# A third output buffer and two moved groups of row sums in a fused attention and mixture-of-experts kernel

## The chip, the cores and the metric

The kernel runs on one core of one Trainium2 chip. The metric is the device time of one execution in microseconds (us); less is better.

## The reference, cut to what matters

```python
# q, k, v: 8 batches, 8 heads, 576 tokens, 64 wide; s: one number per token and head
scores = (q @ k.T) / sqrt(64)                       # causal
scores += minimum(-(cum_i - cum_j), 0)              # cum = cumsum(max(s, 0))
x = softmax(scores) @ v                             # all heads side by side: (4608, 512)
logits = x @ w_gate                                 # 8 experts
# a token keeps the expert of the token before it unless its local gate says "fresh"
e = argmax(logits[t]) if first or sigmoid(x @ w_local) < 0.5 else e_of_the_token_before
out[t] = softmax(logits)[e] * (maximum(x[t] @ w1[e], 0) @ w2[e])   # w1: 512x1024, w2: 1024x512
```

All numbers are 32-bit floats.

## The kernel before, in words

The kernel has two stages. The first, attention with the routing of tokens to experts, takes about the first 205 us. It writes each token's row of x into a table in DRAM that is sorted by expert, with indirect DMAs from GpSimd's queue (`put`, L371). The change doesn't touch it.

The second stage (`Experts`) works through 17 **units**, numbered 0 to 16, in the order `PPDDDDDDDDXTXDMXD`. A unit is a block of rows that belong to one expert: P and D have 256 rows, X is a wide unit of 464 rows, T and M are made of smaller pieces with weights of their own. Each unit has two **phases**: layer 1 (h = relu(x w1)) and layer 2 (y = h w2, times the gate). The phases are interleaved, so that layer 1 of unit u+1 stands between layer 1 and layer 2 of unit u: 1(0), 1(1), 2(0), 1(2), 2(1), and so on, to 1(16), 2(15), 2(16). This document writes 1(13) for layer 1 of unit 13.

Most phases are computed as a 2x2 block product with seven block products instead of eight (`layer_split`, L738 on): all phases of D and X units, and layer 2 of P units. TensorE makes the products in the order p1, p2, p6, p7, p5, p4, p3 (each in a PSUM bank, X units in layer 1 in two). Around them stand these helper operations:

- **Row sums** (`row_sums`, L691): three additions over blocks of the left operand. For x (layer 1) they write the tile xSs and the block a21 of xTs, for h (layer 2) the tile hSs and the block a21 of hT. On GpSimd (POOL) for all but the first units: lines 700, 701, 702. p6 and p5 read the sums, p7 reads the new a21. The tiles hSs and xSs have two halves, used by units of even and odd number in turn; a wide unit takes both halves (`half_of`).
- **The fourth sum** (`row_fourth`, L704, L706): subtracts a sum from the block a12, also on POOL. It can run only when p2 has read the old a12, and p3 needs the new one.
- **Weight sums** (`weight_first` to `weight_fourth`, L655): four subtractions on VectorE (DVE) over blocks of the weights. p5 needs the first, p6 the second, p7 the third, p4 the fourth.
- **The combination** (`add`, L759): DVE adds products from PSUM to running sums. p1 is copied to the tile sa by ScalarE (ACT, L776); p6 gives sb, p7 gives sc; the four results c11, c22, c21, c12 go to hT (layer 1) or to an output tile y (layer 2). ACT then applies relu (L767) or the gate (L763).
- **The stores**: in layer 2 each finished row block of y goes to DRAM by an indirect DMA from POOL's queue (`store`, L818 to L825), which waits for ACT. Row block 1 (c21, c22) is stored after p4, row block 0 after p3. A unit takes one y tile, a wide unit two; the pool yp has two buffers, and a buffer is free again when its store has landed.

T and M units are not split in this way: layer 1 is L837, layer 2 L869 with its own product, and the output's scaling by the gate is L871.

The engines run freely and wait for each other by semaphores; each executes its own instructions in the order in which the program issues them. So an instruction that waits on POOL holds up all that stands behind it in POOL's queue. `run` writes this order out by hand: `job(phase, unit, i, f)` puts the helper f of some unit at place i of a phase; place i of a split phase comes after p1 (0), p2 (1), p6 (2), p7 (3), p5 (4), p4 (5) or p3 (6), and "pre" ahead of all. The helper `at(1)` is called right after `row_fourth` has been issued.

In this order the sums of h of unit u stood at place 0 of 1(u+1), and for the last unit, 16, at place 5 of 2(15).

Of the kernel before, what the change touches and what calls it, by code (L numbers as in the profile page):

```python
# [9 lines left out]
F32 = mybir.dt.float32  # L10
# [7 lines left out]
P = 128  # L18
B, H, S, DH = 8, 8, 576, 64
D = H * DH  # L20
E, F = 8, 1024
# [496 lines left out]
class Experts:  # L518
# [172 lines left out]
    def row_sums(self, u, layer):  # L691

        t, s, of = ((self.xT, self.xss, self.xS), (self.hT, self.hss, self.hS))[layer]
        t = t[u]
        n, h = t.shape[1] // 2, self.width(u) // 2
        s = self.half_of(s, u)[:, : 2 * n * h].rearrange("p (i c t) -> p i c t", i=2, c=n)
        s1, s2 = of[u] = [s[:, i] for i in range(2)]
        (a11, _), (a21, a22) = self.rows_of(t, u)
        on = self.adder(u, layer)
        on.tensor_tensor(s1, a21, a22, op=Alu.add)  # L700
        on.tensor_tensor(s2, s1, a11, op=Alu.subtract)  # L701
        on.tensor_tensor(a21, a11, a21, op=Alu.subtract)  # L702
# [35 lines left out]
    def layer_split(self, u, layer, at):  # L738

        nc = self.nc  # L740
        h, w, parts = self.width(u) // 2, D // 2, self.deep(u)
        p = h // parts
        if layer == 0:
            pool = self.hx if self.kind(u) == "X" else self.fp
            self.hT[u] = pool.tile([P, FK, 2 * h], F32, name="hT")
            (c11, c12), (c21, c22) = self.rows_of(self.hT[u], u)
        else:
            gi = self.gi.pop(u)
            ys = [self.yp.tile([P, 2, D], F32, name="y") for _ in range(parts)]
            y = [ys[r] if parts == 2 else ys[0][:, r : r + 1] for r in range(2)]  # L750
            (c11, c12), (c21, c22) = [[y[r][:p, :, i * w : i * w + w] for i in range(2)] for r in range(2)]

        def sums(name):
            s = self.sp.tile([P, FK // 2 * WIDE // 2], F32, name=name)
            return s[:p, : parts * w].rearrange("p (c w) -> p c w", c=parts) if layer else s[:, : 4 * h].rearrange("p (m t) -> p m t", t=h)

        def add(to, ps, s):
            for c, part in ps:
                nc.vector.tensor_tensor(to[:, c], part, s[:, c], op=Alu.add)  # L759

        def gated(to, r):
            for c in range(parts):
                ins = nc.scalar.mul(to[:, c], to[:, c], gi[:p, parts * r + c, 1:2]).ins  # L763
            return ins

        def last(to, r):
            return gated(to, r) if layer else nc.scalar.activation(to, to, Act.Relu).ins  # L767

        def store(r):
            for c in range(parts):  # L770
                self.store(y[r][:, c], gi, parts * r + c, p)

        p1 = self.product(u, layer, 1)
        s1 = sums("sa")
        for c, part in p1:
            ins = nc.scalar.copy(s1[:, c], part).ins  # L776
        at(0, ins)
        p2 = self.product(u, layer, 2)
        add(c11, p2, s1)
        self.weight_fourth(u, layer)  # L780
        self.row_fourth(u, layer)
        at(1, last(c11, 0))
        p6 = self.product(u, layer, 6)
        s2 = sums("sb")
        add(s2, p6, s1)
        at(2)
        p7 = self.product(u, layer, 7)
        s3 = sums("sc")
        add(s3, p7, s2)
        at(3)  # L790
        p5 = self.product(u, layer, 5)
        add(s2, p5, s2)
        add(c22, p5, s3)
        at(4, last(c22, 1))
        p4 = self.product(u, layer, 4)
        add(c21, p4, s3)
        ins = last(c21, 1)
        if layer:
            store(1)
        at(5, ins)  # L800
        end = u == len(self.units) - 1
        if layer and end:
            gated(s2, 0)
        p3 = self.product(u, layer, 3)
        if layer and end:
            for c, part in p3:
                for i in range(c.start, c.stop):
                    ins = nc.vector.scalar_tensor_tensor(c12[:, i], part[:, i], gi[:p, i, 1:2], s2[:, i], Alu.mult, Alu.add).ins
        else:
            add(c12, p3, s2)  # L810
            ins = last(c12, 0)
        if layer:
            store(0)
        at(6, ins)
        for of in ((self.xT, self.xS), (self.hT, self.hS))[layer]:
            of.pop(u)
# [58 lines left out]
    def run(self, recs, wend, out_of):  # L875
        tc, ctx, nc, router = self.tc, self.ctx, self.nc, self.router

        def pool(name, bufs, **kw):
            return ctx.enter_context(tc.tile_pool(name=name, bufs=bufs, reuse_waits="tile", **kw))
# [5 lines left out]
        self.hss = once.tile([P, 2 * FK * P], F32, name="hSs")  # L885
        self.xss = once.tile([P, 2 * DK * P], F32, name="xSs")
        self.sp = pool("sp", 1)
        self.yp = pool("yp", 2)
        self.ps = pool("ps", 8, space=PSUM)
        last, first, end = NG - 1, sum(EARLY), len(self.units)  # L890
        self.banks = lambda name: self.bank(name).unsqueeze(1)
# [77 lines left out]
        def job(what, u, i, f, *args):  # L969

            plan(what, u, i if i == "pre" else min(i, steps[self.kind(u)][what - 1] - 1), lambda: f(*args))

        for u in range(end):
            if u >= 2:
                job(2, u - 2, "pre" if u > 2 else 1, turn_x, u)
            for layer in range(2):
                if not self.split(u, layer):
                    continue
                if layer:
                    places = (2, u - 1, 5), (1, u + 1, "pre"), (1, u + 1, 2)  # L980
                    if u == 0:
                        places = (1, 1, 6), (1, 1, 7), (1, 1, 7)
                    elif u == 1:
                        places = (2, 0, 5), (1, 2, 1), (1, 2, 3)
                    elif self.kind(u - 1) == "T":
                        places = (1, u + 1, 6), (1, u + 1, 6), (2, u, "pre")
                    place = (1, u + 1, 0) if u + 1 < end else (2, u - 1, 5)
                    if u < 2:
                        place = ((1, 1, "pre"), (2, 0, 2))[u]
                    job(*place, self.row_sums, u, 1)  # L990
                else:
                    places = (1, u - 1, 5), (2, u - 2, "pre"), (2, u - 2, 2)
                    if self.kind(u - 1) == "T":
                        places = (2, u - 2, 5), (2, u - 2, 6), (1, u, 0)
                    elif self.kind(u - 2) == "T":
                        places = ((2, u - 2, "pre"),) * 3
                    elif u == 2:
                        places = (2, 0, 4), (2, 0, 5), (1, 2, 0)
                    job(2, u - 2, 1 if self.kind(u - 2) in "DX" else "pre" if u > 2 else 3, self.row_sums, u, 0)
                for f, place in zip((self.weight_first, self.weight_second, self.weight_third), places):  # L1000
                    job(*(place if place[1] < end else (2, u, "pre")), f, u, layer)
            if self.kind(u) in "MT":
                for r, place in enumerate(((2, u - 1, 1), (2, u - 1, 3), (1, u + 1, 2), (1, u + 1, 3))):
                    job(*place, self.turn_h, u, r)
# [996 lines left out]
```

## Time and profile before

| what | us |
|---|---|
| median of three timed runs (697.57, 700.55, 701.0) | 700.55 |
| the profiled execution | 695.5 |
| its span on the core | 693.8 |
| TensorE busy | 666.8 |
| VectorE busy | 496.5 |
| GpSimd busy | 369.0 |
| ScalarE busy | 195.0 |

The profile is one execution, taken with the hardware profiler. In its rows PE is TensorE, DVE VectorE, ACT ScalarE, POOL GpSimd and SP SyncE. A row of a timeline has the start in us from the span's start, the duration, the engine, the line, the operation, output <- inputs, shapes, the count of merged instructions, and in brackets how long the engine had been idle before it and what ended that. A matmul over 32-bit floats is two instructions, so a block product is 16 instructions in layer 1, and in layer 2 it is 8 for a 256-row unit and 16 for a wide one.

### The profile page before, as it was taken

The page shows a single profiled execution, that of the slowest core. Times are in us where ns is not written, and L with a number is a line of the kernel's source. Part 1 is how long each engine was busy: PE and PEld are TensorE (multiplying, and loading weights), DVE is VectorE, ACT ScalarE, POOL GpSimd, SP SyncE. Part 2 cuts the span into 40 slices and gives each one's busy share as a digit, 9 for nine tenths or more (in the row PEclk, how much of TensorE's full clock was granted, in tenths as well). Part 3 has the DMA queues.
Part 4 walks back from the last instruction along what each step waited for, and adds up shares of the span by engine and source line. Part 5 has one row for each costly group of instructions (what it writes and reads, how often), then busy time and mean ns, then how long its engine had stood idle before and what let it go on. Part 6 is the DMA issues. An engine that isn't in the chain of part 4 may idle for free.

```text
span 693.8 us, 18443 instructions
## 1 busy us (share of the span) xinstructions
PE 666.8 (96%) x7501; PEld 573.5 (83%) x7501; DVE 496.5 (72%) x940; ACT 195.0 (28%) x353; POOL 369.0 (53%) x523
## 2 busy tenths in 40 slices
PE   8999989989999999999999999999999999899995
PEld 6887877867888899999999999996797886696774
DVE  4565856877976898978988998765558555477743
ACT  4555535535522112122221212212121102111111
POOL 3552476766745878946457456714531616306335
PEclk9999999999999999999999999999999999899999
DMA  7664665756659788489968473709858796523002
GB/s 261 187 194 135 208 199 150 224 191 205 203 142 395 242 320 280 167 307 330 325 246 289 147 203 139 286 3 344 278 183 316 303 294 222 152 108 136 0 18 70
DMA packets 56533, 145.75 MB, mean 210 GB/s; under 512 B 13088, under 2 KB 33952, under 8 KB 51448
## 3 DMA queue, kind: packets, MB, share of 16 engines
q1 hardware_dynamic: 47352, 124.23, 54.3%
q0 software_dynamic: 8992, 20.11, 8.1%
q8 instruction: 61, 1.00, 0.6%
q14 instruction: 32, 0.26, 0.1%
q10 hardware_dynamic: 96, 0.15, 0.1%
HBM read 123.83 MB, written 20.85 MB: 209 GB/s over the span
## 4 chain that ended last, share of the span: by engine, by line
PE 78%; issue 7%; POOL 5%; DMA 4%; DVE 4%; SPq 0%; ACT 0%; POOLq 0%; DVEq 0%
PE p L727 24%; PE p L734 21%; PE ps L1199 10%; PE po L1256 6%; PE pb L1256 6%; PE hp L846 3%; DMA out_dram<-y,gi 3%; PE yp L869 2%; POOL out_dram L821 2%; PE lp L238 1%; PE ph L1217 1%; POOL hT L702 1%; DMA w1b<-in_w_dram 1%; PE hp L837 1%; PE po L1268 1%
## 5 line engine op out<-in xcount | busy, mean ns | idle before, releaser
L734 PE MATMUL p<-w2b,hT 128*128 128x256 f32 (+1 forms) x720 | 166.1, 384 | 3.6 <-DVE w2b L655 3.4
L734 PEld LDWEIGHTS p<-w2b,hT 128*128 128x128 f32 (+1 forms) x720 | 135.0, 189 | 27.3 <-issue 3.8
L727 PE MATMUL p<-xTs,w1b 128*128 128x128 f32 (+1 forms) x1040 | 143.5, 295 | 2.7 <-POOL xTs L706 2.4
L727 PEld LDWEIGHTS p<-xTs,w1b 128*128 128x128 f32 x1040 | 138.1, 191 | 6.8 <-POOL xTs L706 2.7
L1200 ACT ACTIVATE e<-ps 128x768 f32<-128x768 f32 (+1 forms) x96 | 76.4, 886 | 65.0 <-PE ps L1199 48.8
L821 POOL DMA_INDIRECT out_dram<-y,gi x38 | 48.1, 1265 | 83.4 <-ACT y L763 75.4
L763 ACT ACTIVATE y<-y,gi 128x256 f32<-128x256 f32 (+1 forms) x71 | 34.5, 505 | 171.9 <-DVE y L759 152.9
L767 ACT ACTIVATE hT<-hT 128x512 f32<-128x512 f32 (+1 forms) x52 | 36.8, 711 | 145.0 <-DVE hT L759 145.0
L1199 PE MATMUL ps<-qb,kb 64*128 64x384 f32 (+4 forms) x516 | 76.7, 442 | 0.8 <-DMA kb<-in_k_dram 0.5
L1199 PEld LDWEIGHTS ps<-qb,kb 64*128 64x128 f32 x516 | 47.4, 187 | 27.7 <-ACT e L1200 10.3
L706 POOL TENSOR_TENSOR hT<-hT,hSs 128x512 f32<-128x512 f32 (+1 forms) x15 | 22.4, 1492 | 87.5 <-PE p L734 87.4
L734 PE MATMUL p<-wt,hSs 128*128 128x256 f32 (+1 forms) x288 | 67.2, 379 | 1.3 <-POOL hSs L701 1.3
L371 POOL DMA_INDIRECT table<-xb,idx x54 | 57.6, 1066 | 15.4 <-issue 14.1
L734 PEld LDWEIGHTS p<-wt,hSs 128*128 128x128 f32 (+1 forms) x288 | 53.7, 187 | 10.1 <-POOL hSs L701 1.7
L727 PE MATMUL p<-xSs,wt 128*128 128x128 f32 (+1 forms) x416 | 58.9, 295 | 0.5 <-DVE wt L655 0.5
L727 PEld LDWEIGHTS p<-xSs,wt 128*128 128x128 f32 x416 | 55.6, 192 | 1.2 <-PE p L727 0.7
L1183 POOL TENSOR_SCALAR_AFFINE_SELECT e<-e 128x128 f32<-128x128 f32 (+1 forms) x96 | 35.5, 393 | 38.5 <-ACT e L1200 38.1
L1256 PE MATMUL pb<-vg,e 128*64 128x66 f32 x1280 | 42.4, 223 | 6.3 <-issue 6.3
L1256 PEld LDWEIGHTS pb<-vg,e 128*64 128x64 f32 x1280 | 40.0, 138 | 7.4 <-issue 7.2
L1256 PE MATMUL po<-vg,e 128*64 128x66 f32 x1280 | 41.9, 223 | 1.9 <-issue 1.8
L1256 PEld LDWEIGHTS po<-vg,e 128*64 128x64 f32 x1280 | 39.2, 138 | 3.6 <-issue 2.3
L1176 DVE TENSOR_TENSOR vg<-va,wk 128x256 f32<-128x256 f32 x64 | 37.6, 653 | 0.0
(298 smaller groups left out, 941.3 us busy)
## 6 DMA issues: line engine op xcount, KB each, us to landing
w2b<-in_w_dram SPq DMA_DIRECT2D x20, 2048.0 KB, 12.4
w1b<-in_w_dram SPq DMA_DIRECT2D x19, 2048.0 KB, 11.1
va<-in_v_dram SPq DMA_DIRECT2D x32, 320.0 KB, 4.0
xq<-table SPq DMA_DIRECT2D x72, 130.0 KB, 8.3
kb<-in_k_dram SPq DMA_DIRECT2D x31, 288.0 KB, 4.3
qb<-in_q_dram SPq DMA_DIRECT2D x31, 288.0 KB, 3.2
w1b<-in_w_dram SPq DMA_DIRECT2D x4, 512.0 KB, 4.7
table<-xb,idx POOLq DMA_INDIRECT x54, 4.9
```

Of the source, the lines that this page charges most:

```text
L371: put = self.nc.gpsimd.indirect_dma_start(out=self.halves, in_=src, element_offset=0, in_offset=None, out_offset=bass.IndirectOffsetOnAxis ...
L706: self.adder(u, layer).tensor_tensor(a12, a12, (self.xS, self.hS)[layer][u][1], op=Alu.subtract)
L727: mm(ps[:, m * h : m * h + h], lhsT=b[:, k, (c * of + m) * P : (c * of + m) * P + P], rhs=a[:, k, :], start=m == 0 and k == 0, stop=m == o ...
L734: mm(ps[:p, c * w : c * w + w], lhsT=a[:, k, c * p : c * p + p], rhs=b[:, k, :], start=c == 0 and k == 0, stop=c == parts - 1 and k == n - 1)
L763: ins = nc.scalar.mul(to[:, c], to[:, c], gi[:p, parts * r + c, 1:2]).ins
L767: return gated(to, r) if layer else nc.scalar.activation(to, to, Act.Relu).ins
L821: put = nc.gpsimd.indirect_dma_start(out=self.out[:, :], out_offset=bass.IndirectOffsetOnAxis(ap=gi.bitcast(I32)[:m, n, 0:1], axis=0), in_ ...
L1176: nc.vector.tensor_tensor(vg[:, to].rearrange("p c h e -> p (c h) e")[:, :, :DH], va[:, :c].rearrange("p c h e -> p (c h) e"), wk[:, n, to ...
L1183: nc.gpsimd.affine_select(out=ap, in_=ap, compare_op=Alu.is_ge, fill=0.0, base=base, pattern=n, channel_multiplier=-1)
L1199: mm(ps[:, h, at : at + z - a], lhsT=kb[d, key : key + P], rhs=qb[d, a:z], start=True, stop=True)
L1200: exps[n, u] = nc.scalar.activation(e[:, :, : WIDTH[u]], ps, Act.Exp, scale=scale).ins
L1256: of = mm(po[part][d, j - a, :], lhsT=weights_of(n, c, j, h), rhs=vgs[n % NV][:, c if j < 2 * G1 else G1 + c, h, :], start=(first and i == ...
```

## The change

The pool yp gets three buffers. To make room, the tile sc goes: the sum that p7 makes is written to the buffer of sa (one buffer, whose earlier content was last read when p6's sum was made). The sums of h of a wide unit move from place 0 to place 1 of the next unit's layer 1, which is behind that unit's fourth sum of x; the wide units are 10, 12 and 15. The sums of h of the last unit move from place 5 to place 0 of 2(15), and write to a buffer of their own (the pool hsp, whose tile the M unit used for its h), since the wide unit 15 holds both halves of hSs until its p5.

```diff
@@ row_sums
-        s = self.half_of(s, u)[:, : 2 * n * h].rearrange("p (i c t) -> p i c t", i=2, c=n)
+        if layer and u == len(self.units) - 1:
+            s = self.hsp.tile([P, F], F32, name="hs")
+        else:
+            s = self.half_of(s, u)
+        s = s[:, : 2 * n * h].rearrange("p (i c t) -> p i c t", i=2, c=n)
@@ layer_split
-        s3 = sums("sc")
+        s3 = sums("sa")
@@ run
-        self.yp = pool("yp", 2)
+        self.yp = pool("yp", 3)
...
-                    place = (1, u + 1, 0) if u + 1 < end else (2, u - 1, 5)
+                    place = (1, u + 1, int(self.deep(u) > 1)) if u + 1 < end else (2, u - 1, 0)
```

Line numbers from L700 on are four higher in the changed kernel.

**POOL's queue from the store of unit 14 on.** These are the rows of before, in the phases 1(16), 2(15) and the start of 2(16). The first is unit 14's store; xTs and the shape with 2x128 belong to unit 16's x, hT with 928 or 4x232 to unit 15, hT with 512 or 4x128 to unit 16.

```order
L821 DMA out_dram<-y,gi 4608x512
L700 TENSOR_TENSOR hSs<-hT 128x928
L701 TENSOR_TENSOR hSs<-hSs,hT 128x928
L702 TENSOR_TENSOR hT<-hT 128x4x232
L706 TENSOR_TENSOR xTs<-xTs,xSs 128x2x128
L706 TENSOR_TENSOR hT<-hT,hSs 128x4x232
L820 MEMSET gap 1x1
L821 DMA out_dram<-y,gi 4608x512
L820 MEMSET gap 1x1
L821 DMA out_dram<-y,gi 4608x512
L700 TENSOR_TENSOR hSs<-hT 128x512
L701 TENSOR_TENSOR hSs<-hSs,hT 128x512
```

And the same place now:

```order
L825 DMA out_dram<-y,gi 4608x512
L710 TENSOR_TENSOR xTs<-xTs,xSs 128x2x128
L704 TENSOR_TENSOR hSs<-hT 128x928
L705 TENSOR_TENSOR hSs<-hSs,hT 128x928
L706 TENSOR_TENSOR hT<-hT 128x4x232
L704 TENSOR_TENSOR hs<-hT 128x512
L705 TENSOR_TENSOR hs<-hs,hT 128x512
L706 TENSOR_TENSOR hT<-hT 128x4x128
L710 TENSOR_TENSOR hT<-hT,hSs 128x4x232
```

Unit 16's fourth sum of x has moved ahead of unit 15's three sums of h, and unit 16's three sums of h have moved ahead of unit 15's fourth sum of h and of its first two stores. At 1(13) the same exchange is made between unit 13's fourth sum of x and unit 12's sums of h. At the third wide unit, 10, the rows stand in the same order as before: the T unit that follows it has no fourth sum.

**VectorE's queue at the start of 2(13).** Rows of before, with the semaphores that each waits for: DMASW are those of stores and other indirect DMAs, DMAHW those of loads. The second row writes c11 of unit 13 into a y tile, the third is the fourth weight sum, which p4 needs, and the fourth turns rows of unit 14's h.

```order
L655 TENSOR_TENSOR wt_6796<-w1b,wt_6796 128x1024
L759 TENSOR_TENSOR y<-p_6824,sa 128x256 [waits DMASW1_49,DMASW2_49,PE_49,Activation_49]
L655 TENSOR_TENSOR w2b<-w2b,wt_6743 128x4x256
L855 STREAM_TRANSPOSE hT<-hs 32x8x32 x4
L759 TENSOR_TENSOR sb<-p_6841,sa 128x256 [waits PE_49]
```

And now:

```order
L655 TENSOR_TENSOR wt_6796<-w1b,wt_6796 128x1024
L763 TENSOR_TENSOR y<-p_6824,sa 128x256 [waits DMASW0_49,PE_49,Activation_49]
L655 TENSOR_TENSOR w2b<-w2b,wt_6743 128x4x256
L859 STREAM_TRANSPOSE hT<-hs 32x8x32 x4
L763 TENSOR_TENSOR sb<-p_6841,sa 128x256 [waits PE_49]
```

No row has moved. Semaphores 1 and 2 were those of the two stores of unit 12's row block 1, semaphore 0 is that of the single store of unit 11, one unit earlier. In the same way c11 of unit 16 waited for the two stores of unit 15's row block 1, and waits now for the store of unit 14.

**TensorE's queue at the end of 2(15).** Rows of before: p4 of unit 15, a small product g_total that counts values out of range, and p3 of unit 15.

```order
L734 MATMUL p_7196<-w2b,hT 116x256 [waits DVE_49,PE_49]
L734 MATMUL p_7196<-w2b,hT 116x256 x7
L1449 MATMUL g_total<-g_count,r_ones 128x1 [waits PE_49]
L734 MATMUL p_7226<-w2b,hT 116x256 [waits Pool_49]
L734 MATMUL p_7226<-w2b,hT 116x256 x7
```

And now:

```order
L738 MATMUL p_7200<-w2b,hT 116x256 [waits DVE_49,PE_49]
L738 MATMUL p_7200<-w2b,hT 116x256 x7
L1453 MATMUL g_total<-g_count,r_ones 128x1 [waits DMASW4_49,DMASW3_49,DMASW5_49,DMASW2_49,DMASW6_49,DMASW1_49,DMASW7_49,DMASW0_49,PE_49]
L738 MATMUL p_7227<-w2b,hT 116x256 [waits Pool_49]
L738 MATMUL p_7227<-w2b,hT 116x256 x7
```

The order is the same; g_total has got waits for all eight semaphores of the indirect DMAs. In the built program the counts that it waits for are 144 and 160, which eight of the stores to the table (L371) bring about; the first two stores of unit 15 raise theirs to 240.

## The prediction

> **What bounds the kernel now.** I read the page's head first, then the chain of waits, then TensorE's timeline from 525 us to the end, and last the other engines where TensorE stands still.
>
> ```profile
> span 693.8 us, 18443 instructions
> ```
>
> The profiled execution took 695.5 us, 1.7 more than its span. The chain of waits shows what a phase costs where nothing disturbs it, and one long transfer:
>
> ```profile
> 310.53 12.09 PE p L734 x56
> 322.62 12.50 PE p L727 x112
> ...
> 577.70 17.59 DMA out_dram<-y,gi
> ```
>
> An undisturbed layer 2 of a 256-row unit (L734) takes 12.09 us, a layer 1 (L727) 12.50, start to start, and TensorE runs through both without a pause. Time can be won where it pauses or is slow. These are the rows of its timeline at the phases with pauses:
>
> ```profile
> 539.84 3.84 PE L727 MATMUL p<-xTs,w1b 128*128 128x128 f32 x32
> 551.61 2.05 PE L727 MATMUL p<-xTs,w1b 128*128 128x128 f32 x16 [0.79 <-POOL xTs L706]
> 553.50 7.07 PE L734 MATMUL p<-w2b,hT 128*116 128x256 f32 x32
> 584.78 3.72 PE L734 MATMUL p<-w2b,hT 128*128 128x256 f32 x16
> 597.12 6.41 PE L734 MATMUL p<-w2b,hT 128*128 128x256 f32 x16 [3.44 <-DVE w2b L655]
> 603.37 6.43 PE L727 MATMUL p<-xTs,w1b 128*128 128x232 f32 x32
> 632.41 3.84 PE L727 MATMUL p<-xTs,w1b 128*128 128x128 f32 x32
> 645.50 2.05 PE L727 MATMUL p<-xTs,w1b 128*128 128x128 f32 x16 [1.57 <-POOL xTs L706]
> 647.38 7.07 PE L734 MATMUL p<-w2b,hT 128*116 128x256 f32 x32
> 668.25 7.14 PE L734 MATMUL p<-w2b,hT 128*116 128x256 f32 x32
> 676.69 1.99 PE L734 MATMUL p<-wt,hSs 128*128 128x256 f32 x8 [1.30 <-POOL hSs L701]
> 682.45 3.62 PE L734 MATMUL p<-w2b,hT 128*128 128x256 f32 x16
> ```
>
> Four phases are longer than an undisturbed one. 1(13), from 539.84 to 553.50, takes 13.66: **1.16** too much. 2(13), from 584.78 to 603.37, takes 18.59: **6.50** too much. 1(16), from 632.41 to 647.38, takes 14.97: **2.47** too much. 2(16) begins half way through the row at 668.25 (its 32 instructions are p3 of unit 15 and p1, p2 of unit 16), so at 671.82, and ends at 686.07: 14.25, or **2.16** too much. Each pause names its cause: the fourth sum of x for 1(13) and 1(16), a weight sum for 2(13), the sums of h for 2(16).
>
> The pause in 2(13) is 3.44, yet the phase loses 6.50. The granted clock tells the rest (columns: stretch, its length, PE busy, clock, share of the DMA engines, GB/s):
>
> ```profile
> 588.00:593.60 5.60, 5.60 (x27) 1.00 1.01 374
> 594.00:598.00 4.00, 0.88 (x2) 0.73 0.67 100
> 598.00:602.00 4.00, 4.00 (x11) 0.50 0.00 0
> 602.00:606.00 4.00, 4.00 (x20) 0.92 0.37 94
> ```
>
> After the pause TensorE gets half its clock, so that p4 and p3 took 6.41 instead of the 3.62 of the same products in the row at 682.45: 2.79 more.
>
> **The change part by part.**
>
> *Third y buffer: the whole loss of 2(13).* Why the weight sum was late is in VectorE's timeline:
>
> ```profile
> 579.61 1.22 DVE L655 TENSOR_TENSOR w2b<-w2b 128x1024 f32<-128x1024 f32 x1
> 595.42 0.42 DVE L759 TENSOR_TENSOR y<-p,sa 128x256 f32<-128x256 f32 x1 [7.35 <-DMA out_dram<-y,gi]
> 672.58 2.94 DVE L655 TENSOR_TENSOR wt<-w2b,wt 128x1024 f32<-128x1024 f32 x1
> 675.44 2.28 DVE L655 TENSOR_TENSOR w2b<-w2b 128x1024 f32<-128x1024 f32 x1
> 679.48 0.42 DVE L759 TENSOR_TENSOR y<-p,sa 128x256 f32<-128x256 f32 x1 [1.76 <-DMA out_dram<-y,gi]
> ```
>
> The write of c11 of unit 13 stood 7.35 us until a store of unit 12, issued at 577.70, had landed, 17.59 later; behind it in VectorE's queue is the fourth weight sum, and p4 waits for that. With three buffers c11 waits for unit 11's store, in POOL's timeline:
>
> ```profile
> 542.43 1.01 POOL L821 DMA_INDIRECT out_dram<-y,gi  x1 [2.61 <-issue]
> ```
>
> Even with 17.59 to land it is home by 561, well ahead of 588. What is late next? The fourth weight sum then follows p2 (two products, 3.5 us into the phase) by 0.42 and 1.22 us, and p4 starts five products in, at 8.6: 3.5 us to spare. So no pause, no slow clock: minus 6.50. The least that this can bring is nothing, if the transfer lands early in a timed run; the most is set by how long stores take:
>
> ```profile
> L821 POOLq EVENT_SEMAPHORE  x13: 17/17/43, 575.8 to 685.5; - x13
> DMA to landing us min/median/max: 3.1/7.5/17.6
> ```
>
> Only a landing in 10.4 us or less would have spared c11 the wait. This one store shared full DMA engines (1.01 above) with weight loads that the program issues at the same place each time, so I take 17.6.
>
> [...]
>
> *Sums of h behind the fourth sum of x.* POOL's timeline at the three places:
>
> ```profile
> 543.46 2.18 POOL L700 TENSOR_TENSOR hSs<-hT 128x928 f32<-128x928 f32 x1
> 548.71 2.16 POOL L702 TENSOR_TENSOR hT<-hT 128x928 f32<-128x928 f32 x1
> 550.82 0.74 POOL L706 TENSOR_TENSOR xTs<-xTs,xSs 128x256 f32<-128x256 f32 x1
> 583.12 1.28 POOL L700 TENSOR_TENSOR hSs<-hT 128x512 f32<-128x512 f32 x1
> 633.59 1.72 POOL L821 DMA_INDIRECT out_dram<-y,gi  x1 [3.07 <-DVE y L871]
> 635.33 2.25 POOL L700 TENSOR_TENSOR hSs<-hT 128x928 f32<-128x928 f32 x1
> 640.64 3.14 POOL L702 TENSOR_TENSOR hT<-hT 128x928 f32<-128x928 f32 x1
> 643.74 1.71 POOL L706 TENSOR_TENSOR xTs<-xTs,xSs 128x256 f32<-128x256 f32 x1
> 671.85 1.27 POOL L821 DMA_INDIRECT out_dram<-y,gi  x1 [0.21 <-issue]
> 674.50 2.13 POOL L701 TENSOR_TENSOR hSs<-hSs,hT 128x512 f32<-128x512 f32 x1
> ```
>
> The three sums of a wide unit held POOL from 543.46 to 550.87 and from 635.33 to 643.78, and the fourth sum, then p3, stood behind them. Now the fourth sum starts when p2 ends (543.68 and 636.25), and is ready at 544.4 and 638.0 at the durations shown, 6 us and more ahead of p3. Behind it the sums of h take the same 7.4 and 8.45, to 552 and 646.5. They are next needed by p6 of 2(12) and 2(15), two products (7.07) after these phases begin at 552.3 and 644.9: at 559.4 and 652. The margin is 7 and 5 us; only beyond it would the move cost, us for us. I take the whole 1.16 and 2.47, since the phases have no other cause of delay in these rows; from below, what the named pauses don't cover could stay, 0.37 (1.16 less 0.79) and 0.90 (2.47 less 1.57). At unit 10 nothing moves: 0.
>
> *Sums of h of the last unit.* They stood behind two stores of unit 15, of which the second was issued at 671.85, and p6 waited for the second of them (674.50 to 676.6). Now they start when ACT has made the last piece of unit 16's h:
>
> ```profile
> 649.36 1.82 ACT L767 ACTIVATE hT<-hT 128x512 f32<-128x512 f32 x3 [9.37 <-DVE hT L759]
> ```
>
> So from 651.2, three of 1.28 to 3.1 each, to 655.0 or 660.5 at worst, 15 us before use. The instruction now queued behind them is unit 15's fourth sum, needed by p3 at 668.25: 5 us to spare at worst after 2.16 (the length of the rows at 543.46 and 548.71, which are as large). The stores behind these move with it, earlier than before. Two things remain for 2(16): c11's wait of 1.76 for a store, which the third buffer takes away, and the weight sums at 672.58 and 675.44. At 2.94 and 2.28 they would be ready for p7 only at 677.8 where it could start at 676.9: 0.9 of the 2.16 stays. At 1.22 (row 579.61) they are ready at 675.1, and p6 can start at 675.3. I take 1.22, since POOL's additions are no longer beside them.
>
> [...]
>
> *sc goes into sa: 0.* p7's sum is written by VectorE, which was also the last to read sa, so order alone does it. ACT's copy of the next phase's p1 must now follow c21's add; but ahead of the copy ACT waits anyway for c12's add, which VectorE makes after c21's.
>
> *g_total's eight waits.* Eight more semaphore instructions on TensorE's queue at 17 to 43 ns (row of L821 above, POOL's): 0 to 0.34, and 0 taken, as the queue is read ahead of the matmuls.
>
> Sum: 1.16 + 6.50 + 2.47 + 2.16 = 12.29, so the profiled execution would take 683.2. The loads and fetches are released by the same phases as before and keep their distance to use. The tail, 7.7 us from TensorE's end to the span's, is unchanged. The timed median, 700.55, is 5.05 above the profiled execution; the trace doesn't show where. I carry the gain over as it is: **688.3**.
>
> **The rivals.**
>
> *Stores land early in timed runs.* The third buffer then brings nothing: 5.79 in all, 694.8. For it: the median landing is 7.5. Against: timed runs are longer than the profiled one, not shorter.
>
> *The clock dips only in the profiled run.* 2(13) gives 3.71, in all 9.5: 691.1. The spread of the timed runs, 3.4, is of that size.
>
> *Only the y wait goes*, since POOL's or VectorE's queue is late elsewhere and gives back 5.8: 694.0. Against: the margins of 5 us and more above.
>
> *g_total's wait is a live one* (slower). TensorE stands at it between p4 and p3 of unit 15. If it had to see unit 15's first two stores land, p3 would start 3.1 to 17.6 us after 673.1 (the second's issue ended), at 7.5 so 680.6 instead of 668.25, and with the dip of 2.8 that is 15.1 lost for 12.3 won: 703.4. It decides from a landing of some 5 us on. Against it: the counts waited for belong to stores to the table, whose last ones are over by 295:
>
> ```profile
> L371 POOL DMA_INDIRECT table<-pad,pad_i x8: 960/1124/2027, 276.2 to 293.6; - x8
> ```
>
> *The change does nothing measurable*: the pauses are refilled by something that the profile puts down to others, 700.5.
>
> **How the numbers follow.** A measurement of this kernel can tell about 0.5% (3.5 us) from no change. Forecast 0.67; no dip 0.08; early landing 0.09; only the y wait 0.10; no effect 0.04; live wait 0.02. All but the last two are faster by over 0.5%, 0.94; of the two at 694 to 695, whose gain is under twice that bound, I put 0.02 to "same". The forecast's own range is 685 to 691. Upwards the whole reaches to 695 for the early landing; downwards to 683.2, where the timed runs' extra 5.05 is the same wait, longer.
>
> **What would show it right or wrong.** Right: TensorE's timeline has 1(13) and 1(16) at 12.5, 2(13) and 2(16) at 12.1 to 12.3, no granted clock of 0.5 near 595, and no VectorE row that waits for out_dram. A pause at L710 or at hs or hSs (L705) would show the sums late; a pause at L1453 the live wait; a y wait that is left would break the largest term.

## The result and the profile after

The changed kernel took 688.38 us (median of four runs, 687.62 to 689.02), the kernel before 699.87 on the same chip (697.57 to 701.0): a ratio of 0.984, 95% interval 0.9811 to 0.9868, or 11.5 us.

The profiled execution of after took 688.37 us. The head of its page:

```profile
span 686.6 us, 18445 instructions
```

So the span fell by 7.2 us only (693.8 before), though the timed gain is 11.5. Where the rest is, two rows of TensorE's timelines tell, the first product of unit 0's layer 1, before and after. All that precedes it is the attention stage, which the change doesn't touch:

```profile
205.78 5.45 PE L846 MATMUL hp<-xTs,w1b 128*128 128x256 f32 x24
```

```profile
210.15 5.45 PE L850 MATMUL hp<-xTs,w1b 128*128 128x256 f32 x24
```

In this execution of after the first stage took 4.37 longer. What follows must therefore be compared from its own start. The profiled execution of before had a lower mean clock (0.993) than that of after (0.998); its 1(13), 1(16) and 2(16), however, have the same lengths, to 0.02 us, in every profile below that leaves them as they were. These are TensorE's rows of after at the four phases (start, duration, line, operands, count; a bracket would give the idle time ahead of the row and what ended it):

```profile
544.13 3.84 PE L731 MATMUL p<-xTs,w1b 128*128 128x128 f32 x32
...
553.16 3.74 PE L731 MATMUL p<-xTs,w1b 128*128 128x128 f32 x32
556.74 7.07 PE L738 MATMUL p<-w2b,hT 128*116 128x256 f32 x32
...
588.02 3.72 PE L738 MATMUL p<-w2b,hT 128*128 128x256 f32 x16
...
596.76 3.62 PE L738 MATMUL p<-w2b,hT 128*128 128x256 f32 x16
600.21 6.43 PE L731 MATMUL p<-xTs,w1b 128*128 128x232 f32 x32
...
629.26 3.84 PE L731 MATMUL p<-xTs,w1b 128*128 128x128 f32 x32
...
638.29 3.74 PE L731 MATMUL p<-xTs,w1b 128*128 128x128 f32 x32
641.86 7.07 PE L738 MATMUL p<-w2b,hT 128*116 128x256 f32 x32
...
662.58 0.28 PE L1453 MATMUL g_total<-g_count,r_ones 128*128 128x1 f32 x2
662.72 7.14 PE L738 MATMUL p<-w2b,hT 128*116 128x256 f32 x32
...
674.88 3.62 PE L738 MATMUL p<-w2b,hT 128*128 128x256 f32 x16
```

No row has a bracket: TensorE pauses nowhere in these phases. From start to start (2(16) begins in the middle of the row at 662.72 and ends with the last row):

| phase | before | after | gain | predicted |
|---|---|---|---|---|
| 1(13) | 13.66 | 12.61 | 1.05 | 1.16 |
| 2(13) | 18.59 | 12.19 | 6.40 | 6.50 |
| 1(16) | 14.97 | 12.60 | 2.37 | 2.47 |
| 2(16) | 14.25 | 12.21 | 2.04 | 2.16 |
| sum | | | 11.86 | 12.29 |

From the start of 1(13) to the end of TensorE's work it was 146.23 before (539.84 to 686.07) and is 134.37 now (544.13 to 678.50): 11.86 again, so nothing was lost between the four. The windows of after, over 2(13), 1(16) and 2(16) (stretch, its length, PE busy, clock, DMA share, GB/s):

```profile
588.00:600.20 12.20, 12.20 (x58) 10.75 (x57) 11.41 (x18) 1.48 (x3) 8.91 (x7) 1.00 1.00 298
629.20:641.80 12.60, 12.60 (x114) 12.55 (x113) 12.37 (x11) 1.22 (x2) 10.19 (x5) 1.00 0.52 187
666.20:678.50 12.30, 12.30 (x57) 10.48 (x56) 8.30 (x10) 3.20 (x7) 5.87 (x8) 1.00 0.30 75
```

PE is busy for the whole of each, at full clock (the columns between are PEld, DVE, ACT and POOL); in the first the DMA engines are as full as ever, and nobody waits for it. VectorE's rows in 2(13) and 2(16):

```profile
591.84 0.42 DVE L763 TENSOR_TENSOR y<-p,sa 128x256 f32<-128x256 f32 x1 [0.52 <-issue]
...
667.06 1.22 DVE L655 TENSOR_TENSOR wt<-w2b,wt 128x1024 f32<-128x1024 f32 x1
668.19 1.22 DVE L655 TENSOR_TENSOR w2b<-w2b 128x1024 f32<-128x1024 f32 x1
669.96 0.42 DVE L763 TENSOR_TENSOR y<-p,sa 128x256 f32<-128x256 f32 x1 [0.55 <-issue]
670.30 3.07 DVE L655 TENSOR_TENSOR w2b<-w2b,wt 128x1024 f32<-128x1024 f32 x1
```

The waits of 7.35 and 1.76 for out_dram are gone, and the two weight sums of 2(16) take 1.22 each instead of 2.94 and 2.28. The overlap did not vanish, though. It moved: the fourth weight sum now takes 3.07, beside unit 16's fourth sum of h on POOL (the last of the rows below). It is ready at 673.4, 1.5 us ahead of p4 at 674.88.

POOL's rows of after around 1(13) and from 1(16) on:

```profile
548.13 0.72 POOL L710 TENSOR_TENSOR xTs<-xTs,xSs 128x256 f32<-128x256 f32 x1 [0.39 <-PE p L731]
548.81 3.13 POOL L704 TENSOR_TENSOR hSs<-hT 128x928 f32<-128x928 f32 x1
...
554.12 2.16 POOL L706 TENSOR_TENSOR hT<-hT 128x928 f32<-128x928 f32 x1
...
633.25 0.89 POOL L710 TENSOR_TENSOR xTs<-xTs,xSs 128x256 f32<-128x256 f32 x1 [1.10 <-PE p L731]
...
640.35 2.37 POOL L706 TENSOR_TENSOR hT<-hT 128x928 f32<-128x928 f32 x1
647.39 1.27 POOL L704 TENSOR_TENSOR hs<-hT 128x512 f32<-128x512 f32 x1 [4.67 <-ACT hT L771]
...
671.01 1.27 POOL L710 TENSOR_TENSOR hT<-hT,hs 128x512 f32<-128x512 f32 x1
```

The fourth sums of x start when p2's last product releases them, 4.0 us into each phase. The wide units' sums of h are done at 556.3 and 642.7; p6 of the following layer 2 starts at 563.64 and 648.77, so the margins are 7.4 and 6.0 us where 7 and 5 were forecast.

1(16) of before had one more pause, of 0.29, which the prediction's rows don't show. These are that pause and the weight sum that ended it, and the same weight sum in after:

```profile
641.91 2.02 PE L727 MATMUL p<-xTs,w1b 128*128 128x128 f32 x16 [0.29 <-DVE w1b L655]
```

```profile
639.19 2.57 DVE L655 TENSOR_TENSOR w1b<-w1b,wt 128x1024 f32<-128x1024 f32 x1
```

```profile
634.07 1.22 DVE L655 TENSOR_TENSOR w1b<-w1b,wt 128x1024 f32<-128x1024 f32 x1
```

So moving POOL's sums helped VectorE as well. That they had lengthened its weight sum is argued from their running at the same time, not shown.

### The profile page after: what moved, and what is told of

Read it like the earlier page. It is cut to its first block, busy times and chain, and to the rows that moved or that the text cites. A ratio compares the mean times of both kernels' runs of the same rounds, so it can differ in the third digit from the quotient of the medians.

```text
span 686.6 us, 18445 instructions
## 1 busy us (share of the span) xinstructions
PE 666.2 (97%) x7501; PEld 574.0 (84%) x7501; DVE 492.6 (72%) x940; ACT 195.4 (28%) x353; POOL 369.1 (54%) x523
## 4 chain that ended last, share of the span: by engine, by line
PE 88%; issue 5%; DVE 3%; POOL 2%; ACT 1%; POOLq 0%; DVEq 0%
PE p L738 26%; PE p L731 26%; PE ps L1203 11%; PE po L1260 6%; PE pb L1260 6%; PE hp L850 4%; PE yp L873 2%; PE hp L841 2%; PE ph L1221 2%; PE lp L238 2%; POOL out_dram L825 1%; PE po L1272 1%; DVE wt L655 1%; PE pb L1272 1%; PE warm L1127 1%
## 5 line engine op out<-in xcount | busy, mean ns | idle before, releaser
L738 PE MATMUL p<-w2b,hT 128*128 128x256 f32 (+1 forms) x720 | 163.0, 379 | 0.0
L738 PEld LDWEIGHTS p<-w2b,hT 128*128 128x128 f32 (+1 forms) x720 | 133.3, 187 | 22.0 <-PE hp L841 1.6
L371 POOL DMA_INDIRECT table<-xb,idx x54 | 57.4, 1063 | 15.2 <-issue 13.4
L738 PE MATMUL p<-wt,hSs 128*128 128x256 f32 (+1 forms) x272 | 63.3, 379 | 0.0
L738 PEld LDWEIGHTS p<-wt,hSs 128*128 128x128 f32 (+1 forms) x272 | 50.7, 186 | 8.0
L763 DVE TENSOR_TENSOR hT<-p,sa 128x512 f32<-128x512 f32 (+1 forms) x48 | 31.2, 667 | 33.6 <-PE p L731 33.6
```

The lines of the kernel that those rows point to most:

```text
L371: put = self.nc.gpsimd.indirect_dma_start(out=self.halves, in_=src, element_offset=0, in_offset=None, out_offset=bass.IndirectOffsetOnAxis ...
L738: mm(ps[:p, c * w : c * w + w], lhsT=a[:, k, c * p : c * p + p], rhs=b[:, k, :], start=c == 0 and k == 0, stop=c == parts - 1 and k == n - 1)
```

## The experiments

Two theories stood against each other. The prediction's: four pauses with three separate causes, so that the gains add up. The rival: the pauses hang together, so that one part of the change moves them all, or moves one only to lengthen another. Four kernels ran beside the kernel before on one chip, where that took 691.19 (median of 21 runs, 686.17 to 696.89). In brackets stand the names by which the kernels are called further on.

**The third buffer alone (y3_only).** Before, with

```diff
-        s3 = sums("sc")
+        s3 = sums("sa")
-        self.yp = pool("yp", 2)
+        self.yp = pool("yp", 3)
```

> The third y buffer and the sum in sa, with both groups of row sums at their old places. Theory (the four losses are separate and add up): 2(13) falls from 18.59 us to about 12.2, 1(13) and 1(16) stay at 13.7 and 15.0, 2(16) stays between 13.5 and 14.3 because the sums of h are still late; the time is 6.4 to 7.0 us below the kernel before, about 693.2. Rival (the losses hang together, one late queue moving from place to place): 2(13) gets shorter, but 1(16) or 2(16) grows by more than 1 us, and the gain is under 5 us.

Measured: 685.13, a ratio of 0.9911 to the kernel before (95% interval 0.9889 to 0.9933), or 6.1 us, a little under the 6.4 to 7.0 expected. TensorE's rows:

```profile
581.21 3.72 PE L734 MATMUL p<-w2b,hT 128*128 128x256 f32 x16
...
593.40 6.43 PE L727 MATMUL p<-xTs,w1b 128*128 128x232 f32 x32
...
635.52 2.05 PE L727 MATMUL p<-xTs,w1b 128*128 128x128 f32 x16 [1.56 <-POOL xTs L706]
...
666.72 1.99 PE L734 MATMUL p<-wt,hSs 128*128 128x256 f32 x8 [1.30 <-POOL hSs L701]
```

2(13) is 12.19, undisturbed. The two other pauses stand as before (1.57 and 1.30): 1(13) is 13.64, 1(16) 14.97, 2(16) 14.26. The buffer acts on 2(13) alone.

**The moved sums alone (moves_only).** Before, with two y buffers and sc kept, and

```diff
+        if layer and u == len(self.units) - 1:
+            s = self.hsp.tile([P, F], F32, name="hs")
-                    place = (1, u + 1, 0) if u + 1 < end else (2, u - 1, 5)
+                    place = (1, u + 1, int(self.deep(u) > 1)) if u + 1 < end else (2, u - 1, 0)
```

> Both groups of row sums moved, the last unit's in a buffer of their own, with two y buffers and sc kept. Theory: 1(13) and 1(16) fall to 12.6, 2(13) keeps a loss of about 6.4 us with a pause of about 3.4 and the slow clock behind it; 2(16) loses its wait for the sums but c11's wait for a store becomes the last one there, so that it ends between 12.2 and 13.0; the gain is 4.5 to 5.5 us. Rival (the rival 'only the y wait goes' of the prediction): the gain is under 2 us, as the moved sums come late somewhere else.

Measured: 686.81, ratio 0.9931 (0.9898 to 0.9964), 4.4 us. The gain is just under the 4.5 to 5.5 expected. 1(13) and 1(16) both fell to 12.61, as expected. In 2(13) the pause stayed, 3.35, but this time without a slow clock, and the phase took 15.78. The miss is 2(16): 14.08, not 12.2 to 13.0. Rows of TensorE, POOL and VectorE:

```profile
592.49 3.69 PE L738 MATMUL p<-w2b,hT 128*128 128x256 f32 x16 [3.35 <-DVE w2b L655]
...
672.49 3.69 PE L738 MATMUL p<-w2b,hT 128*128 128x256 f32 x16 [1.64 <-DVE w2b L655]
```

```profile
662.14 1.27 POOL L825 DMA_INDIRECT out_dram<-y,gi  x1 [0.21 <-issue]
```

```profile
670.79 0.42 DVE L763 TENSOR_TENSOR y<-p,sa 128x256 f32<-128x256 f32 x1 [5.57 <-DMA out_dram<-y,gi]
```

p6 no longer waits for sums of h. But the write of c11 came to its place sooner and stood 5.57 us until the store issued at 662.14 had landed, 8.65 later. Behind it the fourth weight sum was late, and p4 waited 1.64 for that. So in 2(16) the sums and the y buffer are two waits that end nearly together. Removing either wins 0.2 or nothing (14.08 and 14.26 against 14.25), removing both wins 2.04. Here the rival is right: this term does not split between the two edits.

**sc into sa alone (sa_only).** Before, with `s3 = sums("sa")` only.

> Only p7's sum goes to the buffer of sa; two y buffers, no moved sums. Theory: nothing, within 0.5 us stage by stage, since the order of VectorE and ScalarE already keeps the writers behind the readers. Rival (one buffer ties ScalarE's copy of the next p1 to c21's add): the split phases of 256-row units get longer by 0.1 to 0.5 us each, 3 to 12 us in all.

Measured: 690.98, ratio 0.9977 (0.9949 to 1.0005): no difference. 1(13), 1(16) and 2(16) are 13.65, 14.96 and 14.26. 2(13) is 17.64 instead of 18.59, with a pause of 3.57, and p4 and p3 are slowed less than before (why, the last experiment tells):

```profile
594.39 5.33 PE L734 MATMUL p<-w2b,hT 128*128 128x256 f32 x16 [3.57 <-DVE w2b L655]
```

**The weight loads held back (hold_loads).** The prediction said that the store landed late because it shared the DMA engines with weight loads. If that is so, two buffers are enough when the loads aren't there. Before, with two loads of 2 MB (w2 for the second piece of matrices, w1 for unit 16) put behind 2(13) in the program:

```diff
-            if now:
+            if now and (what, u) not in ((2, 12), (1, 14)):
                 loads(now)
```

> The kernel before with two y buffers and no other part of the change, but the two weight loads of 2 MB that were issued at 577.87 and 584.88 us are held back until after 2(13). Theory (the store of unit 12 took 17.6 us to land because it shared full DMA engines with these loads): it lands in about 8 us, c11 of unit 13 waits for nothing, 2(13) takes about 12.2, the other three phases stay long, and the gain is about 6.4 us, unless the held loads come late for the M unit's layer 2 or for 1(16). Rival (the landing is long for another reason, such as the store's own many short rows): the store still lands after 15 us or more and 2(13) keeps its loss.

Measured: 684.26, ratio 0.9906 (0.9878 to 0.9934), 6.9 us. The DMA view over unit 12's four stores, in the kernel before (577 to 595) and in this one (572 to 584), issue, count and the median from issue to landing:

```profile
w2b<-in_w_dram SPq DMA_DIRECT2D x1, 2048.0 KB, 11.0
w1b<-in_w_dram SPq DMA_DIRECT2D x1, 2048.0 KB
...
out_dram<-y,gi POOLq DMA_INDIRECT x4, 16.0
...
```

```profile
w2b<-in_w_dram SPq DMA_DIRECT2D x1, 2048.0 KB, 8.1
...
out_dram<-y,gi POOLq DMA_INDIRECT x4, 6.7
...
```

The loads were not gone, but late: they went out at 583.48 and 584.68, which is 3.8 and 5.0 us into 2(13) rather than after it. By then the four stores, issued from 570.85 to 576.03, had landed. They took 6.5 to 6.9 us, a median of 6.7 instead of 16.0, and VectorE's c11 in 2(13) waits for none of them:

```profile
583.49 0.42 DVE L759 TENSOR_TENSOR y<-p,sa 128x256 f32<-128x256 f32 x1 [0.52 <-issue]
```

2(13) is 12.19 and the three other phases are as before (13.65, 14.98, 14.25). The long landing is shown to come from the loads, and the store was the whole cause of the pause in 2(13). The four stores of before say the same: the first, issued at 575.96, 1.9 us ahead of the load at 577.87, landed in 7.4 us, the three others in 15.5 to 17.6. This edit and the third buffer are two ways to the same 6 us.

**When a pause is paid for twice (pause_short, pause_mid, pause_long).** moves_only paused 3.35 and lost no clock; before paused 3.44 and lost 2.79. The theory: a pause as short as moves_only's costs nothing on top, and one as long as before's or longer may cost up to about 2.8, whatever its length. The rivals: the slow clock grows with the pause, or it comes from busy DMA engines. Three kernels put the pause back into 2(13) of after, with work on VectorE ahead of the fourth weight sum (five, six and eight reductions):

```diff
+        if layer and u == 13:
+            for _ in range(5):
+                nc.vector.tensor_reduce(self.spare, self.weights(u, layer)[1][1], axis=AX, op=Alu.max)
         self.weight_fourth(u, layer)
```

> The changed kernel with five extra reductions on VectorE ahead of the fourth weight sum of 2(13), so that TensorE pauses there again, about 2.0 us by 1.1 us a reduction; they read weights and write a small spare tile. [...] Rival (any pause there costs clock, in proportion): a granted clock under 0.9 in the 4 us behind it, and 1 us or more beyond the pause.

> As pause_short, with six reductions, a pause of about 3.1 us. [...] Rival: a dip of more than 1 us beyond the pause, as the kernel before had behind 3.44 us.

> As pause_short, with eight reductions, a pause of about 5.3 us. Theory: a dip to about half the clock, and with it 2.8 us or a little more beyond the pause: 2(13), with what of the next phase falls in the slow time, is 20 to 21 us. Rival (the dip of the kernel before had another cause, such as the full DMA engines beside it): no dip, about 17.5.

Each ran once, on another chip: 690.9, 694.75 and 700.59 us, where the kernel before took 698.39. A reduction took 1.25 us (6.23 for the five of pause_short) rather than the 1.1 estimated (weight sums of 128x1024 start 1.13 apart, at 667.06 and 668.19 in the rows of after), so the pauses came out longer than named: 2.76, 4.01 and 6.52. TensorE's p4 and p3 in the three:

```profile
599.45 3.69 PE L738 MATMUL p<-w2b,hT 128*128 128x256 f32 x16 [2.76 <-DVE w2b L655]
```

```profile
601.45 5.38 PE L738 MATMUL p<-w2b,hT 128*128 128x256 f32 x16 [4.01 <-DVE w2b L655]
```

```profile
606.85 5.66 PE L738 MATMUL p<-w2b,hT 128*128 128x256 f32 x16 [6.52 <-DVE w2b L655]
```

All pauses of this case in 2(13), with what p4 and p3 took beyond the 3.69 that they take behind a pause at full clock (the other columns are explained below):

| kernel | pause | least work in a stretch | slow time | work in it | p4 and p3 longer by |
|---|---|---|---|---|---|
| pause_short | 2.76 | 1.92 | 0 | | 0 |
| moves_only | 3.35 | 1.65 | 0 | | 0 |
| before | 3.44 | 1.28 | 6.8 | 5.51 | 2.72 |
| sa_only | 3.57 | 0.00 | 3.4 | 3.32 | 1.64 |
| pause_mid | 4.01 | 1.17 | 3.4 | 3.41 | 1.69 |
| pause_long | 6.52 | 0.00 | 6.8 | 3.98 | 1.97 |

Nothing up to 3.35; 1.6 to 2.7 from 3.44 on, and not more for 6.52 than for 3.57. This looks like a border between 3.35 and 3.44, but the times of the clock's changes tell otherwise. In before it fell at 595.81, rose 6.82 us later at 602.63 and fell again 88.75 after that, at 691.38: 2 and 26 times 3.41. To set the kernels side by side I cut each trace into stretches of 3.41 from a place where its own clock fell, in moves_only from 679.65, after its last product. That the clock changes only at the ends of such stretches is assumed in this, not shown. The stretches around the pause in before and in moves_only, and the one ahead of the fall in pause_mid (stretch, its length, PE busy, clock, DMA share, GB/s):

```profile
592.40:595.81 3.41, 1.28 (x6) 1.00 1.04 185
595.81:602.63 6.82, 5.51 (x13) 0.50 0.11 19
```

```profile
587.49:590.90 3.41, 1.65 (x8) 1.00 1.06 228
590.90:594.31 3.41, 1.82 (x9) 1.00 0.39 74
```

```profile
599.21:602.62 3.41, 1.17 (x6) 1.00 0.49 85
```

In before the clock fell at 595.81, when the pause was only 2.13 old; the stretch that ended there held 1.28 of work. The pause of moves_only, only 0.09 shorter, fell nearly half and half into two stretches, which held 1.65 and 1.82, and the clock stayed. The closest cases on either side stand at the end of the kernel, in hold_loads (the clock stayed) and in pause_short (it fell at 683.29):

```profile
673.10:676.52 3.42, 1.47 (x7) 1.00 0.46 147
```

```profile
679.88:683.29 3.41, 1.39 (x7) 1.00 0.23 83
```

So in the stretches shown the clock fell behind 1.17, 1.28 and 1.39 us of TensorE work and stayed behind 1.47, 1.65 and 1.82. The two whole traces of before and after agree: of their 398 stretches at full clock it fell behind the one with 1.28 and behind two without work after the last product, and behind none of the others, the least of which held 1.49. The slow time lasted one stretch or two, and its price was half of the work that fell into it: half of 5.51, 3.32, 3.41 and 3.98 is 2.76, 1.66, 1.71 and 1.99, beside the 2.72, 1.64, 1.69 and 1.97 measured. In pause_long this was paid with the DMA engines all but idle (a share of 0.02):

```profile
604.00:610.83 6.83, 3.98 (x10) 0.50 0.02 5
```

So both rivals fall. The price didn't grow with the pause, and it didn't come from busy DMA engines: the clock stayed behind a stretch with a DMA share of 1.06 and fell behind one with 0.49. The theory is right in that a longer pause didn't cost more (1.97 behind 6.52, 2.72 behind 3.44), and wrong in the border: 2.13 us of idle time were enough in before, and 3.35 were not in moves_only. As an estimate from these rows, with the stretches as assumed, a pause of 2.0 us (3.41 less 1.39) could already be punished if it lies within one stretch, and one of up to 3.9 (3.41 less 1.47, twice) could pass if a stretch's end halves it.

## Why the prediction was right

- **Its four terms** came out as 1.05, 6.40, 2.37 and 2.04, each 0.10 to 0.12 under the figure. These phases stay at 12.2 and 12.6, not at the 12.09 and 12.50 of the undisturbed rows that it subtracted. That is all that it overshot by: 0.43 of 12.29. That the time came out within 0.1 us of 688.3 is partly luck: the kernel before was 0.7 lower when it was measured again (699.87 for 700.55), and the timed gain was 0.8 smaller than forecast (11.5 for 12.29).
- **Third buffer, whole loss of 2(13).** Shown: y3_only removes it alone. That the store is late because of weight loads is shown by hold_loads. "What is late next" was nothing, as forecast: the windows have PE busy throughout.
- **Sums of h behind the fourth sum of x.** Shown by moves_only for 1(13) and 1(16), both at 12.61. What the named pauses don't cover (0.37 and 0.90) went with them, as taken, but the prediction's "no other cause of delay" overlooked the pause of 0.29 in 1(16). The rest is 0.1 of the undisturbed length and about 0.26 for each pause: elsewhere a row starts 0.16 to 0.17 before the one ahead of it has ended, behind a pause it doesn't, and it takes 0.1 longer (1.99 for 1.89, 2.05 for 1.95).
- **2(16).** The size held, 2.04 for 2.16, and both conditions that it named were needed: early sums, and the third buffer for c11. What it did not see is how nearly they tie. Its 1.76 wait for the store stood there as something that "remains", and I took it in moves_only to cost little; it grew to 5.57 when the sums no longer held the phase up. The instructions of 2.94 and 2.28 fell to 1.22, the value taken. That POOL's additions beside them had lengthened them is argued from overlap in time, and no run shows it. The prediction's "1.28 to 3.1" for each of POOL's sums mixes two shapes: in before, rows of 128x512 took 1.28 with no weight sum beside them (583.12) and 2.13 and 2.25 beside one (674.50, 676.60), but at 673.15 also 1.27 beside one; rows of 128x928 took 2.16 (548.71) and, beside one, 3.03 and 3.14 (545.71, 640.64).
- **sc into sa, and g_total.** sa_only shows the first at nothing. No pause stands at L1453 in after, and p3 follows at once: nothing, as taken, and the rival of 703.4 falls. That the queue is read ahead of the matmuls is seen there too: four semaphore instructions of L1453, 51 ns each, stand at 658.7 to 659.0, its weight load at 662.4.
- **The slow clock in 2(13).** As a price of each execution this step was too firm: the clock fell 2.13 into the pause of before, and executions with 3.35, 3.44 and 3.57 paid 0, 2.72 and 1.64. So the term is worth 3.6 to 6.4, by execution; the rival "the clock dips only in the profiled run" was right in that it can be absent. No run shows its 3.71, which is 6.50 less 2.79; in moves_only the pause without the slow clock cost 3.59 (15.78 for 12.19). In many of the timed runs it seems to have been there, as an estimate: the mean granted clock of the 21 runs of before is 0.9942, that of the ten runs of y3_only and hold_loads, which have no pause there, 0.9969. The difference is 1.9 us of lost clock a run, where one slow stretch loses 1.7 and two lose 3.4. After the change no pause is left to be punished.
- **The 5.05 between the profiled and the timed runs.** The prediction carried it over without knowing where it was. The attention stage, whose length it didn't look at, varies: unit 0's layer 1 began at 205.78 in the profile of before and at 210.15 in that of after. With that stage as long in the profile of before as in that of after, its time would have been 695.5 + 4.4 = 699.9, the median that it was then measured at. That this is where the timed runs' extra lies is argued from the profiled executions; timed runs leave no trace.

So 688.3 was met by the sum as it was made, with the 5.05 carried over unexplained. The early landing, the lost margins on POOL and the live wait fall by after's rows. How all of it adds up: y3_only won 6.1, moves_only 4.4, together 10.5, and after 11.5. The intervals allow an exact sum, but the stages don't: from the start of 1(13) on each won 6.4 (139.82 and 139.83 for 146.23), 12.8 against 11.86. In moves_only's 6.4 are 2.81 of 2(13), the slow clock that its shorter pause happened not to pay, which y3_only wins too; and of 2(16)'s 2.04, 1.87 needs both. The ten timed runs of moves_only have a mean clock of 0.9947, so many of them seem to have paid what its profile did not; that would be why they won 4.4 and not 6.4.

## What to carry to other kernels

Ask of each wait that you remove which other wait on the same path ends just before it: where two nearly tie, either edit alone shows nothing and both together show the gain, so an edit isn't refuted by its own null result. Here a buffer that comes free with a store was late when two loads of 2 MB were issued beside the store (a median landing of 16.0 us for 6.7), and another buffer and a later load were equally good cures (6.1 and 6.9 us). And a profile's span compares only from the place that the edit can touch: here a stage far ahead of it, 4.4 us longer, hid over a third of the gain of 11.9. What a pause costs in clock, too, could not be read from one profile here: pauses of 3.35 and 3.44 us cost 0 and 2.72.

## What was not expected of the hardware

- The price of a pause didn't follow its length: 0 at 3.35 us, 2.72 at 3.44, 1.97 at 6.52. In before the clock fell 2.13 into the pause. In the stretches of 3.41 us shown above it fell behind those with 1.17, 1.28 and 1.39 us of TensorE work and stayed behind those with 1.47, 1.65 and 1.82; in 2(13) it then granted 0.50 for 3.4 or 6.8 us.
- The same four stores landed in a median of 16.0 us beside two loads of 2 MB, and in 6.7 when the loads came later.
- The start of unit 0's layer 1 lay between 200.71 and 202.94 us in the four profiles taken on one chip and between 209.04 and 212.31 in the three on another, though their code up to there does the same work; the kernel before took 691.19 on the first chip and 698.39 on the second. So much of the difference between the chips seems to lie in the attention stage. What in it varies was not tried.
